# Sliding-window attention with sinks and a top-128 MLP: TensorE's order written by hand, five rotating PSUM banks, early row stores, block-wise ranks, indirect DMA

## The chip, the cores and the metric

The kernel runs on one core of one Trainium2 chip. The metric is the device time of one execution in microseconds (us); lower is better. A core has five engines that run beside each other and wait for each other by semaphores: PE (TensorE, matmuls; its weight loads are shown as PEld), DVE (VectorE), ACT (ScalarE), POOL (GpSimd) and SP (SyncE, which only issues DMAs here). DMAs issued by SP appear in the profile as queue q1 (hardware_dynamic), those issued by POOL as queue q0 (software_dynamic); both run on the same 16 DMA engines.

## What is computed

Four batches (B=4), eight heads, 768 positions, head size 64. First attention, in which each query sees the first 4 keys (sinks) and the last 128 keys; then, per batch, the 128 rows with the highest gate score go through a two-layer MLP and are added back:

```python
keep = is_sink | in_window                       # 4 sinks, window of 128
a = softmax(where(keep, q @ k.T / sqrt(64), -1e9))
x = (a @ v) with the heads side by side          # [4, 768, 512]
scores = x @ w_gate
out = x.copy()
for b in range(4):
    top_idx = the 128 rows with the highest scores[b]
    ye = relu(x[b, top_idx] @ w1) @ w2           # 512 -> 1024 -> 512
    out[b, top_idx] += sigmoid(scores[b, top_idx])[:, None] * ye
```

## The kernel before, in words

The work is cut into 24 units (b, j): batch b, and block j of 128 queries, j = 0 to 5. A block's keys are its own block and the one before it, and the sinks.

- `load_qk` (L68) loads q and k of a batch as bf16 through POOL's DMA queue (qb, kb), `load_v` (L82) loads v (vbuf, six chunks of 256 KB, one per block c) and the sink rows (vsk, eight small pieces). For batch 0, POOL issues q and k in four parts each (L77) and then the six chunks of v (L90); the later v loads are issued by SP.
- `transposes` (L136) turns two heads of kb and qb with 24 matmuls against an identity into PSUM (trp, L145); DVE copies the half with k to KT (L150), ACT the half with q to QT (L152).
- `scores` (L160): eight matmuls per block (L169), for block 0 also mask matmuls (L176); ACT takes the exponential into pt (L179); POOL cuts the window edges by affine selects (L182, L186).
- `pv_sinks` (L198) and `pv` (L207): matmuls with pt as weights and vbuf as the moving operand (L214), with the sinks added by two matmuls (L203); DVE divides (L220, L221) into the tile x, which holds a whole batch.
- `finish_block` (L225): DVE's gate scores (L227) and ACT's bf16 copy xb (L230).
- `moe_gen` (L233), the top-128 part of the batch before, is a Python generator advanced during the units of the next batch: scores are spread over all partitions by a diagonal and a ones matmul (dg L240, bc L241, sbc L243), each block's scores are compared with all 768 (cjunk L250), which gives ranks and a selection matrix E (L253) and its transpose ET (L259, L260); selected rows are gathered by 24 matmuls (xeT L267), the MLP follows (hps L284, hT L286, ye L290, gye L293), six matmuls scatter it back (ops L298), DVE adds x (o_sb L300), and SP stores the whole batch (L303).

Unit u issues the scores of unit u+1, then its own pv, then the transposes for the next batch (units j = 1 to 4). The program text gives these as priorities only: a scheduler sets the order of each engine's instructions and mixes them finely. PSUM has eight banks: two buffers of two banks shared by trp, sc, sk, bc, hps and ops, three buffers for xg, one bank for etp, xeT, se and ye. After the last unit the whole generator of batch 3 runs with nothing beside it.

The order of the work is the loop at the end (L323 to L349), of which these lines matter most:

```python
        if nxt:
...
            for g in range(2):
                scores(states[nxt[0]], nxt[1], g)
        pv_sinks(st, j)
        for g in range(2):
            pv(st, j, g)
            if gen is not None:
                if next(gen, "end") == "end":
...
        finish_block(st, j)
...
        if b + 1 < B and 1 <= j <= HP:
            transposes(states[b + 1], j - 1)
```

## Time and profile before

| | us |
|---|---|
| median of 3 runs | 204.23 (202.47 to 204.92) |
| the profiled execution | 201.09 |
| its span, first to last instruction | 199.4 |
| outside its span | 1.69 |
| PE busy | 157.9 (79%) |
| DVE busy | 121.6 (61%) |
| mean granted clock of TensorE | 0.955 |

The rows below come from that one profiled execution. A row of the timeline gives the start, the time until its last instruction has ended, the engine, the line and the instructions merged into it; the time between the starts of two successive PEld rows is what a group takes of PE's queue.

### The profile page before, as it was taken

The numbers are of one execution on the slowest core, as the hardware profiler recorded it, in microseconds if no ns is written. First come the engines' busy times: TensorE is split into PE (matmuls) and PEld (weight loads), VectorE is DVE, ScalarE is ACT, GpSimd is POOL, SyncE is SP. The second block draws the span as 40 slices with busy tenths as digits, with TensorE's granted clock in tenths as the row PEclk, the third lists the DMA queues.
The fourth block names the chain that finished last, engine by engine and source line by source line (L and its number), as shares of the span: only waits on it lengthen the run. The fifth ranks groups of instructions, "written<-read, shape, count | busy, mean of one in ns | idle before, by whom it ended". The sixth has DMA issues, their size and how long they took to land.

```text
span 199.4 us, 5721 instructions
## 1 busy us (share of the span) xinstructions
PE 157.9 (79%) x2456; PEld 109.7 (55%) x2456; DVE 121.6 (61%) x328; ACT 85.9 (43%) x113; POOL 65.7 (33%) x111
## 2 busy tenths in 40 slices
PE   0023998999997999999979999999799999426640
...
PEclk9999999999999999999999999999978999955995
DMA  5999999999999782480400003500000034000016
GB/s 85 188 230 218 200 191 200 201 197 193 190 191 192 129 182 36 154 271 6 105 5 0 3 0 132 190 0 3 0 3 0 3 140 179 5 0 0 0 64 252
DMA packets 33065, 21.63 MB, mean 108 GB/s; under 512 B 19728, under 2 KB 28944, under 8 KB 33040
## 3 DMA queue, kind: packets, MB, share of 16 engines
...
## 4 chain that ended last, share of the span: by engine, by line
PE 52%; DVE 20%; DMA 9%; POOL 7%; ACT 6%; issue 3%; DVEq 1%; ACTq 0%; POOLq 0%
PE xg L214 18%; DVE cjunk L250 11%; DMA kb<-in_k_dram 9%; PE xg L203 6%; PE ye L290 4%; PE bc L241 4%; PE hps L284 4%; PE trp L145 4%; PE xeT L267 4%; DVE E L253 3%; PE sc L169 3%; PE ops L298 3%; POOL vbuf L90 2%; ACT pt L179 2%; POOL qb L77 2%
## 5 line engine op out<-in xcount | busy, mean ns | idle before, releaser
L214 PE MATMUL xg<-vbuf,pt 128*64 128x65 f32 x1408 | 60.8, 231 | 0.0
L214 PEld LDWEIGHTS xg<-vbuf,pt 128*64 128x64 f32 x1408 | 51.2, 142 | 14.4 <-issue 12.3
L182 POOL TENSOR_SCALAR_AFFINE_SELECT pt<-pt 128x512 f32<-128x512 f32 x40 | 25.6, 641 | 92.9 <-ACT pt L179 92.5
L179 ACT ACTIVATE pt<-sc 128x1024 f32<-128x1024 f32 (+1 forms) x48 | 44.8, 953 | 22.2 <-PE sc L169 15.9
L220 DVE RECIPROCAL rz<-xg 128x4 f32<-128x4 f32 x48 | 8.6, 179 | 35.7 <-PE xg L214 35.5
L230 ACT CAST xb<-x 128x512 bf16<-128x512 f32 x24 | 14.8, 616 | 26.2 <-DVE x L221 26.2
L250 DVE TENSOR_SCALAR_CACHE_REDUCE cjunk<-sbc,scol 128x768 f32<-128x768 f32 x24 | 24.1, 1005 | 2.6 <-ACT sbc L243 2.6
L145 PE MATMUL trp<-ident_b,kb 128*64 128x128 bf16 x192 | 10.2, 244 | 14.7 <-DVE ident_b L104 13.6
L186 POOL TENSOR_SCALAR_AFFINE_SELECT pt<-pt 128x512 f32<-128x512 f32 x32 | 21.0, 656 | 0.0
L221 DVE TENSOR_TENSOR x<-xg,rz 128x256 f32<-128x256 f32 x48 | 20.2, 422 | 1.2
L169 PE MATMUL sc<-QT,KT 64*128 64x256 bf16 (+1 forms) x192 | 19.2, 273 | 0.7 <-ACT pt L179 0.2
L203 PE MATMUL xg<-vsk,psk 32*128 32x260 f32 x64 | 19.6, 429 | 0.0
L300 DVE TENSOR_TENSOR o_sb<-ops,x 128x1024 f32<-128x1024 f32 x12 | 14.5, 1220 | 6.4 <-PE ops L298 6.4
L150 DVE COPY KT<-trp 128x768 bf16<-128x768 bf16 x16 | 15.0, 948 | 4.7 <-PE trp L145 4.7
L227 DVE CUSTOM_DVE_ANT_0 junk<-x,wgb 128x512 f32<-128x512 f32 x24 | 16.8, 700 | 0.3
L145 PEld LDWEIGHTS <-kb 128*64 128x64 bf16 x192 | 8.2, 124 | 15.3 <-DMA kb<-in_k_dram 8.0
L259 PE MATMUL etp<-ident_b,E 128*128 128x128 bf16 x24 | 5.9, 244 | 11.0 <-DVE E L253 10.9
L152 ACT COPY QT<-trp 128x768 bf16<-128x768 bf16 x16 | 12.7, 798 | 3.0 <-PE trp L145 2.5
L145 PE MATMUL trp<-ident_b,qb 128*64 128x128 bf16 x192 | 10.2, 244 | 3.6 <-DVE KT L150 3.5
L145 PEld LDWEIGHTS <-qb 128*64 128x64 bf16 x192 | 8.0, 124 | 7.3 <-issue 7.0
L169 PEld LDWEIGHTS <-KT 64*128 64x128 bf16 x192 | 7.0, 95 | 7.9 <-issue 4.7
L203 PEld LDWEIGHTS xg<-vsk,psk 32*128 32x128 f32 x64 | 8.2, 183 | 5.4 <-issue 3.6
...
## 6 DMA issues: line engine op xcount, KB each, us to landing
...
qb<-in_q_dram POOLq DMA_DIRECT2D x3, 768.0 KB, 18.5
kb<-in_k_dram POOLq DMA_DIRECT2D x3, 768.0 KB, 17.1
...
qb<-in_q_dram POOLq DMA_DIRECT2D x4, 192.0 KB, 5.6
kb<-in_k_dram POOLq DMA_DIRECT2D x4, 192.0 KB, 6.0
```

Source lines behind the costliest of these rows:

```text
L145: nc.tensor.transpose(out=trp[64 * e:64 * e + 64, t, c, :], in_=src[:, 2 * hp + e, c, :], identity=ident_b[:])
L150: nc.vector.tensor_copy(out=o, in_=i)
L169: nc.tensor.matmul(out=sc[:, e, hh, 0:nq], lhsT=st.KT[64 * e:64 * e + 64, hp, kc * 128:(kc + 1) * 128], rhs=st.QT[64 * e:64 * e + 64, hp, ...
L179: nc.scalar.activation(out=po[:, :, :, 0:nq], in_=sc[:, :, :, 0:nq], func=ACT.Exp, scale=0.125)
L182: nc.gpsimd.affine_select(out=pt[:, hs, 0:128], in_=pt[:, hs, 0:128], compare_op=ALU.is_ge, fill=0.0, base=0, pattern=[[0, 4], [1, 128]], ...
L186: nc.gpsimd.affine_select(out=pt[:, hs, 128:256], in_=pt[:, hs, 128:256], compare_op=ALU.is_ge, fill=0.0, base=-1, pattern=[[0, 4], [-1, 1 ...
L203: nc.tensor.matmul(out=st.xg[g][:, :, :], lhsT=st.psk[32 * g:32 * g + 32, (j - 2) * 128:(j - 1) * 128], rhs=st.vsk[32 * g:32 * g + 32, :, ...
L214: nc.tensor.matmul(out=xg[64 * m:64 * m + 64, hh, :], lhsT=st.pt[kc][:, h, off + 64 * m:off + 64 * m + 64], rhs=st.v[:, kc, h, :], start=( ...
L221: nc.vector.tensor_tensor(out=st.x[:, j, 256 * g:256 * g + 256].rearrange("p (h d) -> p h d", h=4), in0=xg[:, :, 0:D], in1=rz[:, :, :].to_ ...
L227: nc.vector.tensor_tensor_reduce(out=junk[:, :], in0=st.x[:, j, :], in1=wgb[:, :], scale=1.0, scalar=0.0, op0=ALU.mult, op1=ALU.add, accum ...
L230: nc.scalar.copy(out=st.xb[:, j, :], in_=st.x[:, j, :])
L250: nc.vector.tensor_scalar(out=cjunk[:, :], in0=sbc[:, :], scalar1=scol[:, c:c + 1], scalar2=0.0, op0=ALU.is_gt, op1=ALU.add, accum_out=ran ...
```

## The change

- TensorE's instructions now stand in the order of the program text (`tc.manual_schedule`); the other engines are still ordered by the scheduler.
- One PSUM pool `ps` of five one-bank buffers serves trp (k and q apart), sc (two per half instead of one of two banks), sk, bc, cs, se, xeT, hps (two) and ye in turn; xg keeps three.
- Start: the identity is made before the loads; k is loaded before q; v of batch 0 is issued by SP instead of POOL, and its chunk c = 0 waits for the fifth load of POOL's queue (k of heads 4 and 5). The transposes and scores of batch 0 alternate.
- x is a tile of one block, four buffers, stored to the output as soon as the unit is done (L253). xb is gone.
- Ranks are built block by block: `compare` of unit u-1 runs in unit u and compares block j with blocks 0 to j only; 15 one-column matmuls (cs) sum the rest once per batch.
- The selected rows are gathered from the output in DRAM by an indirect DMA (L309), and the MLP's result is added to them by a second one (L335). ET, the 24 gather matmuls, the six scatter matmuls and o_sb are gone.

```diff
-    sc_ps = ctx.enter_context(tc.tile_pool(name="sc_ps", bufs=2, space=bass.MemoryType.PSUM))
+    ps = ctx.enter_context(tc.tile_pool(name="ps", bufs=5, space=bass.MemoryType.PSUM))
...
-            for src, dst in ((q, st.qb), (k, st.kb)):
-                nc.gpsimd.dma_start(
+            for src, dst in ((k, st.kb), (q, st.qb)):
+                st.loads.append(nc.gpsimd.dma_start(
...
+            ins = nc.sync.dma_start(out=st.v[:, c, :, 0:D],
+                                    in_=v[b, :, c * 128:(c + 1) * 128, :].rearrange("h p d -> p h d"))
+            if behind_load is not None and c == 0:
+                tc.add_manual_dep(ins.ins, behind_load.ins.name, mybir.DependencyInfo(
+                    mybir.DependencyClass.Sync, mybir.DependencyReason.DATA), reason="order of the first loads")
...
+    ident_f = cp.tile([128, 128], FP32, name="ident_f", tag="ident_f")
+    make_identity(nc, ident_f)
     st0 = load_qk(0, 4)
...
+    load_v(st0, st0.loads[4])
...
+            trp = ps.tile([128, 8, 128], BF16, name="trp", tag="ps")
...
+        sc = [ps.tile([128, 2, 256], FP32, name="sc", tag="ps") for _ in range(2)]
...
-        nc.scalar.activation(out=po[:, :, :, 0:nq], in_=sc[:, :, :, 0:nq], func=ACT.Exp, scale=0.125)
+        for e in range(2):
+            nc.scalar.activation(out=po[:, e, :, 0:nq], in_=sc[e][:, :, 0:nq], func=ACT.Exp, scale=0.125)
...
+            st.x = xp.tile([128, DM], FP32, name="x", tag="x")
...
     def finish_block(st, j):
+        nc.sync.dma_start(out=out[st.b, j * 128:(j + 1) * 128, :], in_=st.x[:, :])
...
-        nc.scalar.copy(out=st.xb[:, j, :], in_=st.x[:, j, :])
-
-
-    def moe_gen(st):
+        st.dg = sp.tile([128, 128], FP32, name="dg", tag="dg")
+        nc.vector.tensor_scalar_mul(out=st.dg[:, :], in0=ident_f[:, :], scalar1=st.scol[:, j:j + 1])
...
+    def compare(st, j):
+        bc = ps.tile([128, 128], FP32, name="bc", tag="ps")
+        nc.tensor.matmul(out=bc[:, :], lhsT=ones_f[:, :], rhs=st.dg[:, :], start=True, stop=True)
+        nc.scalar.copy(out=st.sbc[:, j * 128:(j + 1) * 128], in_=bc[:, :])
+        n = 128 * (j + 1)
+        cm = cmp_p.tile([128, n], BF16, name=f"cm{j}", tag=f"cm{j}")
+        nc.vector.scalar_tensor_tensor(
+            out=cm[:, :], in0=st.sbc[:, 0:n], scalar=st.scol[:, j:j + 1], in1=tie[:, S - n:S],
+            op0=ALU.subtract, op1=ALU.is_gt, accum_out=st.row[:, j:j + 1])
+        st.cm[j] = cm
...
+        cs = ps.tile([128, NB], FP32, name="cs", tag="ps")
+        for c in range(NB - 1):
+            for j in range(c + 1, NB):
+                nc.tensor.matmul(out=cs[:, c:c + 1], lhsT=st.cm[j][:, c * 128:(c + 1) * 128],
+                                 rhs=minus1[:, :], start=(j == c + 1), stop=(j == NB - 1),
+                                 skip_group_check=True)
...
+        nc.vector.tensor_tensor(out=st.row[:, 0:nb1], in0=st.row[:, 0:nb1], in1=behind[:, 0:nb1], op=ALU.add)
+        nc.vector.tensor_tensor(out=st.row[:, 0:nb1], in0=cs[:, 0:nb1], in1=st.row[:, 0:nb1], op=ALU.add)
+        E = mp.tile([128, NB, 128], BF16, name="E", tag="E")
+        nc.vector.tensor_tensor(
+            out=E[:, :, :], in0=iota_f[:, :].unsqueeze(1).to_broadcast((128, NB, 128)),
+            in1=st.row[:, :].unsqueeze(2).to_broadcast((128, NB, 128)), op=ALU.is_equal)
...
+        se = ps.tile([128, 2], FP32, name="se", tag="ps")
         for c in range(NB):
-            nc.vector.tensor_scalar(out=cjunk[:, :], in0=sbc[:, :], scalar1=scol[:, c:c + 1],
-                                    scalar2=0.0, op0=ALU.is_gt, op1=ALU.add,
-                                    accum_out=rank[:, c:c + 1])
-            nc.vector.tensor_scalar(out=E[:, c, :], in0=iota_f[:, :], scalar1=rank[:, c:c + 1],
-                                    scalar2=None, op0=ALU.is_equal)
-            if c == 2:
-                yield
-        etp = mo_ps.tile([128, NB, 128], BF16, name="etp", tag="mo")
-        for c in range(NB):
-            nc.tensor.transpose(out=etp[:, c, :], in_=E[:, c, :], identity=ident_b[:])
-        nc.vector.tensor_copy(out=ET[:, :, :], in_=etp[:, :, :])
-        scol16 = mp.tile([128, NB], BF16, name="scol16", tag="scol16")
-        nc.vector.tensor_copy(out=scol16[:, :], in_=scol[:, :])
+            for t in range(2):
+                nc.tensor.matmul(out=se[:, :], lhsT=E[:, c, :], rhs=rd[:, t, c, :],
+                                 start=(c == 0 and t == 0), stop=(c == NB - 1 and t == 1))
+        idx = sp.tile([128, 1], U32, name="idx", tag="idx")
+        nc.vector.tensor_scalar_add(out=idx[:, :], in0=se[:, 0:1], scalar1=float(b * S))
...
+        rows = out[0:b + 1, :, :].rearrange("b s d -> (b s) d")
+        nc.gpsimd.indirect_dma_start(
+            out=xe[:, :], out_offset=None, in_=rows,
+            in_offset=bass.IndirectOffsetOnAxis(ap=idx[:, 0:1], axis=0))
...
+            nc.tensor.transpose(out=xeT[:, dc, :], in_=xe[:, dc * 128:(dc + 1) * 128], identity=ident_b[:])
...
+        nc.gpsimd.indirect_dma_start(
+            out=rows, out_offset=bass.IndirectOffsetOnAxis(ap=idx[:, 0:1], axis=0),
+            in_=gye[:, :], in_offset=None, compute_op=ALU.add)
...
+    with tc.manual_schedule(engines={mybir.EngineType.PE}):
+        start_state(st0)
+        for g in range(2):
+            transposes(st0, 2 * g)
+            transposes(st0, 2 * g + 1)
+            scores(st0, 0, g)
...
+            pv_sinks(st, j)
             for g in range(2):
-                scores(states[nxt[0]], nxt[1], g)
-        pv_sinks(st, j)
-        for g in range(2):
-            pv(st, j, g)
+                pv(st, j, g)
+            if j == 0:
+                sink_scores(st)
+            if b + 1 < B and 1 <= j <= HP:
+                transposes(states[b + 1], j - 1)
+            if u:
+                pb, pj = units[u - 1]
+                compare(states[pb], pj)
             if gen is not None:
                 if next(gen, "end") == "end":
                     gen = None
-        finish_block(st, j)
-        if j == 0:
-            sink_scores(st)
-        if b + 1 < B and 1 <= j <= HP:
-            transposes(states[b + 1], j - 1)
-        if j == NB - 1:
-            gen = moe_gen(st)
-    for _ in gen:
-        pass
+            finish_block(st, j)
+            if j == 0 and b > 0:
+                gen = moe_steps(states[b - 1])
+        compare(states[B - 1], NB - 1)
+        for _ in moe_steps(states[B - 1]):
+            pass
```

The first place is SP's queue at the start of the program. Before, SP loads the gate weights (wgb), the sink rows of batches 0 and 1 (vsk) and then v of batch 1 (vbuf1); v of batch 0 is in POOL's queue:

```order
L131 DMA wgb_162<-in_moe_w_gate_dram 128x512
L88 DMA vsk0_96<-in_v_dram 4x64 [waits DVE_49]
L88 DMA vsk0_96<-in_v_dram 4x64 x6
L88 DMA vsk0_96<-in_v_dram 4x64 [waits DMAHW0_49]
L88 DMA vsk1_97<-in_v_dram 4x64 [waits DMAHW1_49,DVE_49]
```

Now SP's queue holds v of batch 0 (vbuf0_91), the sink rows (vsk0_93), wgb and v of batch 1 (vbuf1_92); DMASW4 is the semaphore of POOL's fifth load, DMAHW0 to DMAHW7 those of SP's own DMAs, in turn:

```order
L88 DMA vbuf0_91<-in_v_dram 128x8x64
L96 DMA vsk0_93<-in_v_dram 4x64 [waits DVE_49]
L96 DMA vsk0_93<-in_v_dram 4x64 x6
L96 DMA vsk0_93<-in_v_dram 4x64 [waits DMAHW0_49]
L88 DMA vbuf0_91<-in_v_dram 128x8x64 [waits DMAHW1_49]
L88 DMA vbuf0_91<-in_v_dram 128x8x64 [waits DMAHW2_49]
L88 DMA vbuf0_91<-in_v_dram 128x8x64 [waits DMAHW3_49]
L88 DMA vbuf0_91<-in_v_dram 128x8x64 [waits DMAHW4_49]
L155 DMA wgb_177<-in_moe_w_gate_dram 128x512 [waits DMAHW5_49]
L88 DMA vbuf0_91<-in_v_dram 128x8x64 [waits DMAHW6_49,DMASW4_49]
L88 DMA vbuf1_92<-in_v_dram 128x8x64 [waits DMAHW7_49]
```

Only the load with the wait for DMASW4 is chunk c = 0: chunks 1 to 5 and wgb moved ahead of it in the queue, since the other engines' order is still the scheduler's.

The second place is PE in batch 1, in unit (1, 1) of the kernel before. There the transposes of the selection matrix (etp) stand between the pv matmuls of one block (xg):

```order
L214 MATMUL xg<-vbuf_95,pt 64x65 x5
L259 LDWEIGHTS E
L259 MATMUL etp<-ident_b,E 128x128
L214 MATMUL xg<-vbuf_95,pt 64x65 x7
L259 LDWEIGHTS E
L259 MATMUL etp<-ident_b,E 128x128
L214 MATMUL xg<-vbuf_95,pt 64x65 x9
```

Now a block's pv stands in one piece, followed by the 24 transposes for the next batch, the spread of one block's scores (bc) and the step of the top-128 part that is due. These rows are the end of unit (1, 1) with the first of the 15 one-column matmuls cs:

```order
L169 MATMUL trp<-ident_b,qb 64x128
L264 MATMUL bc<-dg,ones_f 128x128
L280 LDWEIGHTS cm_608
L280 MATMUL cs<-minus_168,cm_608 128x1
L280 LDWEIGHTS cm_712
L280 MATMUL cs<-minus_168,cm_712 128x1
```

In every unit of batch 1 and later the order is now: eight scores matmuls of the next unit, two sink matmuls, pv, 24 transposes (units 1 to 4, up to batch 2), bc, one step.

The third place is DVE at the end of the program. Before, the six blocks of batch 3 are compared there one after the other, six pairs like the last two rows here, behind the diagonals of the last blocks (dg):

```order
L240 TENSOR_SCALAR dg_2607<-ident_f_130,scol_2035 128x128 [waits DVE_49,PE_49]
L262 CAST scol16_2635<-scol_2035 128x6
L250 TENSOR_SCALAR cjunk_2612,rank_2611<-sbc_2590,scol_2035 128x768 [waits Activation_49]
L253 TENSOR_SCALAR E_2613<-iota_f_160,rank_2611 128x128 [waits DVE_49]
L250 TENSOR_SCALAR cjunk_2612,rank_2611<-sbc_2590,scol_2035 128x768
```

Now DVE ends with the comparisons of blocks 4 and 5 (cm4, cm5), the gate score of block 5 (L255, two instructions), its diagonal, E in one instruction and the row index:

```order
L248 TENSOR_TENSOR x_2704<-xg_2683,rz_2722 128x256 [waits DVE_49]
L268 SCALAR_TENSOR_TENSOR cm4_2728,row_2152<-sbc_2153,scol_2151,tie_159 128x640 [waits Activation_49]
L255 ISA junk_2743,scol_2151<-x_2704,wgb_177 128x512 [waits DVE_49]
L255 ISA scol_2151 128x1
L284 TENSOR_TENSOR row_2152<-row_2152,behind_164 128x5 [waits DVE_49]
L259 TENSOR_SCALAR dg_2745<-ident_f_97,scol_2151 128x128 [waits DVE_49]
L292 TENSOR_SCALAR rid1_174<-scol_2151 128x6
L293 SCALAR_TENSOR_TENSOR rid1_174<-scol_2151,rid1_174 128x6 [waits DVE_49]
L268 SCALAR_TENSOR_TENSOR cm5_2750,row_2152<-sbc_2153,scol_2151,tie_159 128x768 [waits Activation_49]
L285 TENSOR_TENSOR row_2152<-cs_2752,row_2152 128x5 [waits PE_49]
L287 TENSOR_TENSOR E_2770<-iota_f_157,row_2152 128x768 [waits DVE_49]
L302 TENSOR_SCALAR idx_2787<-se_2774 128x1 [waits DMASW3_49,DMASW2_49,PE_49]
```

Four of the six comparisons moved into the units; cm4 stands ahead of the gate score of the last block.

## Rows read from the trace of the kernel before

**Rows 1.** The page, busy time by engine, then the span in 40 slices.

```profile
PE 157.9 (79%) x2456; PEld 109.7 (55%) x2456; DVE 121.6 (61%) x328; ACT 85.9 (43%) x113; POOL 65.7 (33%) x111
...
PE   0023998999997999999979999999799999426640
...
PEclk9999999999999999999999999999978999955995
DMA  5999999999999782480400003500000034000016
```

**Rows 2.** DMA by queue, 24 to 32 us: packets, MB, share of 16 engines.

```profile
q0 software_dynamic: 1491, 1.14, 90.3%
q1 hardware_dynamic: 1496, 0.38, 36.1%
```

**Rows 3.** DMA by queue, 36 to 44 us.

```profile
q1 hardware_dynamic: 1082, 0.27, 26.5%
```

**Rows 4.** DMA by queue, 70 to 75 us.

```profile
q1 hardware_dynamic: 3695, 0.93, 92.6%
```

**Rows 5.** Timeline 0 to 26 us: start, length, instructions, idle before and its releaser.

```profile
7.17 0.13 PEld L145 LDWEIGHTS <-kb 128*64 128x64 bf16 x1 [7.17 <-DMA kb<-in_k_dram]
...
13.60 1.49 PE L145 MATMUL trp<-ident_b,kb 128*64 128x128 bf16 x24 [13.60 <-DVE ident_b L104]
```

**Rows 6.** Timeline 26 to 64 us.

```profile
27.12 1.00 PE L214 MATMUL xg<-vbuf,pt 128*64 128x65 f32 x14
...
33.72 0.53 PE L145 MATMUL trp<-ident_b,kb 128*64 128x128 bf16 x12 [0.65 <-DMA kb<-in_k_dram]
```

**Rows 7.** Timeline 40 to 44.2 us: what each group takes of the weight-load queue.

```profile
40.80 1.95 PEld L214 LDWEIGHTS xg<-vbuf,pt 128*64 128x64 f32 x64 [0.21 <-issue]
...
42.66 0.40 PEld L145 LDWEIGHTS <-kb 128*64 128x64 bf16 x12
...
43.15 0.11 PEld L169 LDWEIGHTS <-KT 64*128 64x128 bf16 x4
...
43.37 0.30 PEld L203 LDWEIGHTS xg<-vsk,psk 32*128 32x128 f32 x4
...
44.01 0.19 PEld L214 LDWEIGHTS xg<-vbuf,pt 128*64 128x64 f32 x2 [0.34 <-issue]
```

**Rows 8.** Chain that ended last, in order of time: start, length, what.

```profile
47.90 0.54 PE sc L176 x2
...
54.92 0.71 PE bc L241 x4
...
71.33 0.63 PE xg L203 x2
72.19 1.81 PE hps L284 x32
...
95.20 0.71 PE bc L241 x4
```

**Rows 9.** Costliest groups: line, shapes, count, busy us, mean ns, idle before.

```profile
L250 DVE TENSOR_SCALAR_CACHE_REDUCE cjunk<-sbc,scol 128x768 f32<-128x768 f32 x24 | 24.1, 1005 | 2.6 <-ACT sbc L243 2.6
...
L150 DVE COPY KT<-trp 128x768 bf16<-128x768 bf16 x16 | 15.0, 948 | 4.7 <-PE trp L145 4.7
L227 DVE CUSTOM_DVE_ANT_0 junk<-x,wgb 128x512 f32<-128x512 f32 x24 | 16.8, 700 | 0.3
```

**Rows 10.** DMA issues by line: KB each, median us to landing.

```profile
kb<-in_k_dram POOLq DMA_DIRECT2D x3, 768.0 KB, 17.1
...
kb<-in_k_dram POOLq DMA_DIRECT2D x4, 192.0 KB, 6.0
```

**Rows 11.** Timeline 168 to 173 us.

```profile
169.25 0.18 DVE L220 RECIPROCAL rz<-xg 128x4 f32<-128x4 f32 x1 [0.29 <-PE xg L214]
```

**Rows 12.** Timeline 177 us to the end.

```profile
181.51 2.72 PE L267 MATMUL xeT<-E,xb 128*128 128x128 bf16 x24 [0.65 <-DVE ET L260]
...
188.17 1.90 PE L290 MATMUL ye<-w_sb,hT 128*128 128x512 bf16 x8 [1.11 <-ACT hT L286]
```

More of the change, by code (lines that the diff above doesn't have):

```diff
@@ L11 @@
 BF16 = mybir.dt.bfloat16
+U32 = mybir.dt.uint32
 ACT = mybir.ActivationFunctionType
@@ L72, in load_qk @@
         st.kb = qkp.tile([128, H, NB, D], BF16, name="kb", tag="kb")
+        st.loads = []
         n = H // parts
@@ L263, in moe_gen @@
+        nc.gpsimd.indirect_dma_start(
+            out=xe[:, :], out_offset=None, in_=rows,
+            in_offset=bass.IndirectOffsetOnAxis(ap=idx[:, 0:1], axis=0))
         yield
-        xeT = mo_ps.tile([128, 4, 128], FP32, name="xeT", tag="mo")
+        xeT = ps.tile([128, 4, 128], BF16, name="xeT", tag="ps")
         for dc in range(4):
-            for c in range(NB):
-                nc.tensor.matmul(out=xeT[:, dc, :], lhsT=st.xb[:, c, dc * 128:(dc + 1) * 128],
-                                 rhs=E[:, c, :], start=(c == 0), stop=(c == NB - 1))
+            nc.tensor.transpose(out=xeT[:, dc, :], in_=xe[:, dc * 128:(dc + 1) * 128], identity=ident_b[:])
@@ L269, in moe_gen @@
         xeT_sb = mp.tile([128, 4, 128], BF16, name="xeT_sb", tag="xeT_sb")
         nc.scalar.copy(out=xeT_sb[:, :, :], in_=xeT[:, :, :])
-        se = mo_ps.tile([128, 4, 128], FP32, name="se", tag="mo")
-        for c in range(NB):
-            nc.tensor.matmul(out=se[:, 0, 0:1], lhsT=E[:, c, :], rhs=scol16[:, c:c + 1],
-                             start=(c == 0), stop=(c == NB - 1))
-        gt = mp.tile([128, 1], FP32, name="gt", tag="gt")
-        nc.scalar.activation(out=gt[:, :], in_=se[:, 0, 0:1], func=ACT.Exp, scale=-1.0)
@@ L277, in moe_gen @@
-        nc.vector.tensor_scalar_add(out=gt[:, :], in0=gt[:, :], scalar1=1.0)
-        nc.vector.reciprocal(out=gt[:, :], in_=gt[:, :])
         yield
         hT = mp.tile([128, 8, 128], BF16, name="hT", tag="hT")
-        hps = sc_ps.tile([128, 8, 128], FP32, name="hps", tag="sc")
-        for fc in range(8):
-            for dc in range(4):
-                nc.tensor.matmul(out=hps[:, fc, :], lhsT=w1_sb[:, dc, fc * 128:(fc + 1) * 128],
-                                 rhs=xeT_sb[:, dc, :], start=(dc == 0), stop=(dc == 3))
@@ L286, in moe_gen @@
-        nc.scalar.activation(out=hT[:, :, :], in_=hps[:, :, :], func=ACT.Relu)
+        for fq in range(2):
+            hps = ps.tile([128, 4, 128], FP32, name="hps", tag="ps")
+            for f4 in range(4):
+                for dc in range(4):
+                    f0 = (4 * fq + f4) * 128
+                    nc.tensor.matmul(out=hps[:, f4, :], lhsT=w1_sb[:, dc, f0:f0 + 128],
+                                     rhs=xeT_sb[:, dc, :], start=(dc == 0), stop=(dc == 3))
+            nc.scalar.activation(out=hT[:, 4 * fq:4 * fq + 4, :], in_=hps[:, :, :], func=ACT.Relu)
@@ L287, in moe_gen @@
         yield
-        ye = mo_ps.tile([128, DM], FP32, name="ye", tag="mo")
+        ye = ps.tile([128, DM], FP32, name="ye", tag="ps")
         for fc in range(8):
@@ L291, in moe_gen @@
                              start=(fc == 0), stop=(fc == 7))
[L292 removed]
+        gye = mp.tile([128, DM], FP32, name="gye", tag="gye")
         nc.scalar.activation(out=gye[:, :], in_=ye[:, :], func=ACT.Copy, scale=gt[:, 0:1])
[L294 to L305 removed]
+        nc.gpsimd.indirect_dma_start(
+            out=rows, out_offset=bass.IndirectOffsetOnAxis(ap=idx[:, 0:1], axis=0),
+            in_=gye[:, :], in_offset=None, compute_op=ALU.add)
```

137 lines of the change are left out of this document (65 added, 72 removed).

## The prediction

> **What bounds the kernel now.** I read the page first (busy times, then the slices), then the DMA queues by window, the timeline of the start, the chain of waits in the middle and the timeline of the end. The page shows PE busy for 157.9 of 199.4 us, with nines from the sixth slice to the thirty-fourth and low digits on both sides [rows 1]: a start of some 27 us, a middle that PE fills, and an end in which PE mostly waits. The DMA row shows nines from the second to the thirteenth slice, so transfers are short of room for the first 65 us.
>
> *Start.* The first k part lands at 7.17, but PE begins at 13.60, when the identity is there [rows 5]; the first pv starts at 27.12 [rows 6]. *Middle.* The spread of batch 0's scores starts at 54.92 and that of batch 1's at 95.20 [rows 8]: 40.28 us for a batch. *End.* The last pv matmul has ended by 169.25 [rows 11]; from there to 199.4 it is 30.2 us, a chain with nothing beside it.
>
> **The start, changed.** The identity now comes first, so PE can begin at about 7 instead of 13.6, and its transposes and scores of batch 0 follow the loads. Then its fixed order brings pv(0, 0), which needs chunk 0 of v. That chunk is the sixth v load of SP's queue, behind chunks 1 to 5, the sink rows and wgb, as the order shows. So its landing time decides, and PE has nothing else that it may do.
>
> How fast does SP's queue move beside POOL's? From 24 to 32 us both had work: 1,491 packets of q0 and 1,496 of q1, one for one, though q0 moved 1.14 MB (765 bytes each) and q1 0.38 MB (256 bytes each, v's rows of one head) [rows 2]. That is 187 packets/us for q1. Beside the larger packets of the weights and q/k it is 1,082 in 8 us, 135/us [rows 3]. Alone it did 3,695 in 5 us, 739/us [rows 4]. Chunk 1 goes first, nearly alone, and I let it land at about 5 us. Behind it stand four chunks and wgb and chunk 0: 5 x 1,024 + 128 = 5,248 packets, from about 6.5 us. POOL's queue holds q and k of batches 0 and 1 (4,096 packets at the 256 per load that 765-byte packets give, some 650 of them gone by then), then w1 and w2. So 3,450 pairs at 187/us take 18.4 us (to 25); the next 1,500 at 135/us 11 us (to 36); the rest alone 0.4 us; with about 1 to 2 us to land, chunk 0 is there at 39 us. Bounds: 22 us if the queues shared evenly by bytes (below), 43 us if all 5,248 went at 135/us. I take 39, since the one-for-one rows are the same situation.
>
> The Trainium skill (DMA: Bandwidth & Descriptors, "Queues, rings and completion order") says that each DMA engine takes turns between its queues packet by packet. The trace agrees (1,491 to 1,496). By that rule alone, chunk 0 lands at the 39 us above; by an even share of bytes it would be near 20.
>
> So the start goes from 27.12 to 39: +12. k and q of batch 1, which PE waits for at 33.72 before [rows 6], are there by then, at no further cost.
>
> **The middle, counted from PE's groups.** From the starts of successive weight loads [rows 7]: 64 pv records (one block) 1.86 us, 12 transposes 0.49, four scores of 128 columns 0.22, the two sink matmuls side by side 0.64; four scores of 256 columns I take at 0.32. From the chain [rows 8]: two masks 0.54, 32 hps 1.81, four bc records 0.71 (so 0.35 for the two of a block). ye takes 1.90 [rows 12]. The four sink-score matmuls I take at 0.87, cs at 0.5, se and the new xeT at 0.4 each (estimates: one-column matmuls and four transposes are below any group of 12 above). A batch in hand order is then, by units 0 to 5: 2.8, 4.3, 4.8, 4.8, 6.1, 6.4, in sum 29.3 us.
>
> The same from above: 40.28 minus what goes, namely 24 gather matmuls (1.5), six etp (1.4), six ops (1.6) and the second half of four sink pairs that stand apart today, 0.63 each [rows 8] (2.5), plus 1.3 for cs, the longer se and the new transposes: 34.6. The gap between the two is the price of mixing (each of the many short pieces of pv pays a change of operand). I take 32: the hand order removes the mixing, but a fixed order waits where the scheduler would have slipped something in. The waits that I see: KT's copy (948 ns [rows 9]) must be done when the third sc buffer of the next unit is taken, about 1.7 us after pv ends by DVE's queue (0.6 for the division, 0.95 for the copy) against 1.6 us by PE's; and xeT must find the gathered rows, 4 to 5 us after se, where PE arrives after 3.5. DVE itself shrinks: six comparisons of 768 (1,005 ns each [rows 9]) become 2,688 columns in all, about 3.5 us for 6.0, and o_sb goes. The two exponentials of 512 per half cost ACT a little more than one of 1,024, and xb pays for it; ACT and POOL (43% and 33% busy [rows 1]) cover both, with one or two us of slack per unit.
>
> Each indirect DMA sits in POOL's queue between affine selects: the gather waits for idx, and behind it stand the selects of the next block, which pv needs. Bounds for its time: 0 beside PE, and 17.1 us, as the 768 KB k loads took [rows 10]; nearest are the 192 KB parts, 6.0 us in full traffic. With DMA quiet after 65 us [rows 1] I take 4, so a batch loses about 1 us to it.
>
> Batch 0 has no top-128 part: 24.3 by the same sums, plus about 2 for waits and for a slow restart (24 transposes took 1.49 us at the start, 12 took 0.53 later [rows 5, 6]): 26.5 for 26.75 before. Batches 1 and 2: 32 each. Batch 3 up to its last pv: 29.3 less its transposes (3.9), next scores (1.7), ye and the last bc (2.2): 21.5; PE is sparser there, and the granted clock fell in such a stretch before (a 7 and an 8 in the PEclk row near 147 us [rows 1]), so I take 25.
>
> **The end.** From the last pv: division 0.8; cm4, which stands ahead of the gate score, 0.9; gate score 0.7 [rows 9] and accumulator 0.1; dg 0.4; bc and its copy 0.7; cm5 1.1; cs and sum 1.0; E 1.1 (0.95 as KT's copy of the same shape); se and idx 0.8; gather 4.0; xeT and copy 1.1; hps 3.0; second hT 0.6; ye 1.9; gye 0.7; scatter and its landing 5.0; the end of the program 0.5. Sum 24.4, for 30.2. hps is put between 1.81 and twice that: after the wait for the gather the PE is cold, as in the end of today, where the clock row shows fives (the lower level, 1.2 GHz) and 24 xeT matmuls took 2.72 us [rows 1, 12]. With the indirect transfers at 2 and at 8.5 the end is 19 to 32.
>
> **The sum.** 39 + 26.5 + 2 x 32 + 25 + 24.5 = 179 us for a span of 199.4. With the 1.69 outside it 180.7 for 201.09. The median of the runs is 204.23, 1.56% above the profiled execution; at that ratio 183.5.
>
> **Rivals.**
> 1. *Chunk 0 is early.* The Trainium skill (same page, "Issuing engines are not separate DMA queues") says that moving transfers between issuing engines saves only the time to issue them. As a mechanism here: 3.4 MB (q, k, v of batch 0, wgb) at the 0.19 MB/us of 1.52 MB in 8 us [rows 2] are 18 us, chunk 0 is there at about 20, PE then waits some 4 us for k and q of batch 1. Span 179 - 39 + 24 = 164, median 168. Against it: the one-for-one packets.
> 2. *No change.* The mixing was not waste and the ends do not shrink: a batch at 36, batch 3 at 29, the end at 30, the rest as above: 196.5 + 1.7, median 201. For it: PE's slices are full in the middle already [rows 1], and a fixed order can't fill a wait.
> 3. *Slower: the five-bank ring.* Every buffer waits for the release of the fifth before it. If DVE runs late by gate score and comparison, KT's copy comes 0.95 + 0.7 + 1.0 = 2.6 us late in each of the 12 units with transposes [rows 9]: +31, span 210, median 215. It decides from 1.7 us per unit on (20.7 us of gain over 12). Against it: DVE's 121.6 us [rows 1] are 30 a batch, and less the 2.5 of the comparisons at most 28 in a batch of 32.
>
> **How the numbers follow.** The forecast's own range is 172 to 196: chunk 0 from 33 to 42, a batch from 29 to 36, the end from 20 to 30. Chances: forecast 0.68, rival 1 0.12, rival 2 0.12, rival 3 0.08. A measurement of this kernel tells about 2% apart. Faster by over 2% (below 200.1): the forecast, rival 1 and a sixth of rival 2: 0.82; within 2% 0.10; slower 0.08. The range that holds 8 in 10 takes in rival 1's time and the middle of rival 2: 168 to 201.
>
> **What would show it.** Right: PE idle from about 19 to 39 us with a wait on a vbuf load; q0 and q1 one for one in that time; bc of equal blocks about 32 us apart in batches 1 and 2; some 24 us from the last pv to the end. Wrong: pv(0, 0) before 28 us (rival 1); waits of PE on KT's copy of over 1 us in every unit (rival 3); waits of pv on the affine selects behind a gather (then the indirect DMA is dearer than 4 us).

## The result and the profile after

The changed kernel takes 187.3 us (median of 4 runs, 186.81 to 188.99), the kernel before 203.35 (200.2 to 204.92): a ratio of 0.932, 95% interval 0.918 to 0.946. The forecast was 183.5 with 168 to 201. The profiled execution took 188.99 us, its span 187.3, with 1.69 outside. Executions that were over 1.5% longer than the shortest of their kernel, at a lower granted clock, are left out of the ratios but not of the medians; the profiled executions of e1, e2, e4 and e8 are of this kind, 2 to 7% above the shortest, so that lengths read from them are somewhat too long.

The page of the kernel after, in the lines that answer to [rows 1]:

```profile
PE 136.1 (73%) x2412; PEld 102.1 (55%) x2412; DVE 103.9 (55%) x313; ACT 76.5 (41%) x161; POOL 76.2 (41%) x117
...
PE   0377400299999994996999979999989789711930
...
PEclk9999999999999997599999978999996969965585
DMA  5999999969999999596406511410241311142004
```

PE works 21.8 us less than before, DVE 17.7 less. The zeros in PE's sixth and seventh slices are the new wait at the start, and the clock row has new dips in the middle (slices 16, 17, 24, 25, 31 and 33). The stages, from the timeline's start of pv in each block 0 and the end of the last pv:

| stage | before | forecast | after |
|---|---|---|---|
| start, to pv(0, 0) | 27.12 | 39 | 36.38 |
| batch 0 | 26.75 | 26.5 | 27.45 |
| batch 1 | 40.28 | 32 | 36.44 |
| batch 2 | 40.28 | 32 | 32.61 |
| batch 3 to its last pv | 34.8 | 25 | 27.19 |
| end | 30.2 | 24.5 | 27.23 |
| span | 199.4 | 179 | 187.3 |

(Batch 3 of before is what the other stages leave.) The start is 9.3 us longer, batches 1 to 3 are 19 us shorter, the end 3 us. PE's waits in the kernel after, by line, what for, total, times and the longest:

```profile
PE xg L239 <- DMA vbuf<-in_v_dram: 15.4, 1, 15.4
PE xeT L315 <- DMA xe<-out_dram,idx: 8.5, 3, 5.3
PE trp L169 <- DMA kb<-in_k_dram: 7.0, 3, 5.5
PE sc L193 <- DVE KT L174: 4.6, 5, 2.6
PE cs L280 <- DVE cm L268: 2.2, 3, 1.3
```

The first is the wait for chunk 0 of v that the prediction describes. In 24 to 32 us the two queues moved as many packets as each other again, as in [rows 2], though not as many bytes (DMA by queue: packets, MB, share of 16 engines):

```profile
q0 software_dynamic: 1000, 1.28, 90.0%
q1 hardware_dynamic: 1000, 0.41, 28.3%
```

Where batch 1 loses 4.4 us against the forecast is seen on PE's and DVE's timelines (start, length, instructions, idle before and its releaser). PE:

```profile
70.56 0.28 PE L193 MATMUL sc<-QT,KT 64*128 64x256 bf16 x1
73.42 1.01 PE L193 MATMUL sc<-QT,KT 64*128 64x256 bf16 x7 [2.58 <-DVE KT L174]
74.36 1.23 PE L228 MATMUL xg<-vsk,psk 32*128 32x260 f32 x4
75.52 3.73 PE L239 MATMUL xg<-vbuf,pt 128*64 128x65 f32 x64
```

DVE at the same place, and in batch 2 at 102 us:

```profile
67.41 1.38 DVE L268 SCALAR_TENSOR_TENSOR cm<-sbc,scol,tie 128x768 bf16<-128x768 f32 x1
...
71.53 0.42 DVE L248 TENSOR_TENSOR x<-xg,rz 128x256 f32<-128x256 f32 x1 [2.08 <-DMA out_dram<-x]
...
102.23 2.62 DVE L255 CUSTOM_DVE_ANT_0 junk<-x,wgb 128x512 f32<-128x512 f32 x1
...
105.35 1.40 DVE L268 SCALAR_TENSOR_TENSOR cm<-sbc,scol,tie 128x768 bf16<-128x768 f32 x1
```

PE stands 2.58 us for KT: DVE could not write x, since the last store of its buffer had not landed, and KT's copy stands behind that. The 64 pv behind this wait take 3.73 us, where an undisturbed block takes 2.09: the granted clock was 0.66 of full speed from 75.5 to 81.5. In batch 2 the same wait on KT is 1.32 us; there junk took 2.62 us instead of 0.69, beside eight affine selects that POOL ran from 101.89 on, behind the scatter.

Batch 1 loses 1.72 us more at the gather, which no store held back: it started 0.44 us after its index did, as in batches 2 and 3, though the profile names a store. It took 5.7 us to land (81.30 to 87.02; the median of the four is 3.8) while the DMA engines were at 0.8 to 0.9 of their time, and PE stood for its rows:

```profile
80.86 0.16 DVE L302 TENSOR_SCALAR idx<-se 128x1 uint32<-128x1 f32 x1
81.30 1.23 POOL L309 DMA_INDIRECT xe<-out_dram,idx  x1 [3.46 <-DMA out_dram<-x]
87.02 0.40 PE L315 MATMUL xeT<-ident_b,xe 128*128 128x128 bf16 x4 [1.72 <-DMA xe<-out_dram,idx]
88.32 2.09 PE L239 MATMUL xg<-vbuf,pt 128*64 128x65 f32 x64
```

The last row shows that the clock does not fall behind every wait: this block took 2.09 us.

The end, PE's timeline from the spread of the last block's scores, which answers to [rows 12]:

```profile
162.78 0.49 PE L264 MATMUL bc<-dg,ones_f 128*128 128x128 f32 x2 [0.49 <-DVE dg L259]
...
166.38 0.48 PE L299 MATMUL se<-rid,E 128*128 128x2 bf16 x12 [1.25 <-DVE E L287]
172.13 0.61 PE L315 MATMUL xeT<-ident_b,xe 128*128 128x128 bf16 x4 [5.27 <-DMA xe<-out_dram,idx]
173.46 3.57 PE L325 MATMUL hps<-xeT_sb,w_sb 128*128 128x128 bf16 x32 [0.73 <-ACT xeT_sb L317]
176.83 2.74 PE L331 MATMUL ye<-w_sb,hT 128*128 128x512 bf16 x8
```

### The profile page after: what moved, and what is told of

It reads as the page before. It is cut to its first block, busy times and chain, and to the rows that moved or that the text cites. A ratio compares the mean times of both kernels' runs of the same rounds, so it can differ in the third digit from the quotient of the medians.

```text
span 187.3 us, 5738 instructions
## 1 busy us (share of the span) xinstructions
PE 136.1 (73%) x2412; PEld 102.1 (55%) x2412; DVE 103.9 (55%) x313; ACT 76.5 (41%) x161; POOL 76.2 (41%) x117
## 3 DMA queue, kind: packets, MB, share of 16 engines
q0 software_dynamic: 11136, 9.96, 34.8%
## 5 line engine op out<-in xcount | busy, mean ns | idle before, releaser
L239 PE MATMUL xg<-vbuf,pt 128*64 128x65 f32 x1408 | 53.6, 242 | 15.4 <-DMA vbuf<-in_v_dram 15.4
L207 POOL TENSOR_SCALAR_AFFINE_SELECT pt<-pt 128x512 f32<-128x512 f32 x40 | 34.1, 863 | 49.6 <-ACT pt L204 49.5
L204 ACT ACTIVATE pt<-sc 128x512 f32<-128x512 f32 (+1 forms) x96 | 46.3, 572 | 9.6 <-PE sc L193 6.8
L211 POOL TENSOR_SCALAR_AFFINE_SELECT pt<-pt 128x512 f32<-128x512 f32 x32 | 28.2, 889 | 0.0
L335 POOL DMA_INDIRECT out_dram<-gye,idx x4 | 6.4, 1604 | 42.8 <-ACT gye L334 42.8
L255 DVE CUSTOM_DVE_ANT_0 junk<-x,wgb 128x512 f32<-128x512 f32 x24 | 20.2, 842 | 0.1
L268 DVE SCALAR_TENSOR_TENSOR cm<-sbc,scol,tie 128x128 bf16<-128x128 f32 (+5 forms) x24 | 18.6, 776 | 1.4 <-ACT sbc L265 0.6
L265 ACT COPY sbc<-bc 128x128 f32<-128x128 f32 x24 | 6.4, 267 | 16.7 <-PE bc L264 16.7
L228 PE MATMUL xg<-vsk,psk 32*128 32x260 f32 x64 | 12.2, 459 | 0.0
L264 PE MATMUL bc<-dg,ones_f 128*128 128x128 f32 x48 | 11.5, 320 | 0.5 <-DVE dg L259 0.5
L259 DVE TENSOR_SCALAR dg<-ident_f,scol 128x128 f32<-128x128 f32 x24 | 10.3, 430 | 0.2
L325 PE MATMUL hps<-xeT_sb,w_sb 128*128 128x128 bf16 x128 | 9.4, 242 | 0.7 <-ACT xeT_sb L317 0.7
```

Source lines behind the costliest of these rows:

```text
L204: nc.scalar.activation(out=po[:, e, :, 0:nq], in_=sc[e][:, :, 0:nq], func=ACT.Exp, scale=0.125)
L207: nc.gpsimd.affine_select(out=pt[:, hs, 0:128], in_=pt[:, hs, 0:128], compare_op=ALU.is_ge, fill=0.0, base=0, pattern=[[0, 4], [1, 128]], ...
L211: nc.gpsimd.affine_select(out=pt[:, hs, 128:256], in_=pt[:, hs, 128:256], compare_op=ALU.is_ge, fill=0.0, base=-1, pattern=[[0, 4], [-1, 1 ...
L228: nc.tensor.matmul(out=st.xg[g][:, :, :], lhsT=st.psk[32 * g:32 * g + 32, (j - 2) * 128:(j - 1) * 128], rhs=st.vsk[32 * g:32 * g + 32, :, ...
L239: nc.tensor.matmul(out=xg[64 * m:64 * m + 64, hh, :], lhsT=st.pt[kc][:, h, off + 64 * m:off + 64 * m + 64], rhs=st.v[:, kc, h, :], start=( ...
L255: nc.vector.tensor_tensor_reduce(out=junk[:, :], in0=st.x[:, :], in1=wgb[:, :], scale=1.0, scalar=0.0, op0=ALU.mult, op1=ALU.add, accum_ou ...
```

## The experiments

Theory: the late chunk 0 alone sets the start; the order by hand saves the price of mixing; batch 1 is held by late stores, by DVE and POOL, and by the low clock behind waits; the end by the gather. The rivals stand in the expectations. Ratios are to the kernel before, timed on the same chip beside each.

**e1, e2: the start.** e1 lets chunk 0 go first; e2 also puts wgb ahead of it.

```diff
+    wgb = cp.tile([128, DM], FP32, name="wgb", tag="wgb")
+    nc.sync.dma_start(out=wgb[:], in_=moe_w_gate.partition_broadcast(128))
-    load_v(st0, st0.loads[4])
+    load_v(st0)
...
```

> The changed kernel, but chunk 0 of v of batch 0 no longer waits for the fifth load of POOL's queue: it is the first load of SP's queue, and wgb the last of them, behind chunk 5. Theory (the late chunk 0 alone sets the start, 36.38 us, and q0 and q1 share packet by packet): pv(0, 0) starts at about 21.5, since chunk 0 is there at about 8; but wgb now lands where chunk 0 did, at about 36, and bc of unit (0, 0), which stands in PE's fixed order in unit (0, 1) (44.19 in the changed kernel), waits for it until about 37.5. So some 6 to 7 us are gained, about 181 us, with a new wait of some 8 us of PE on dg. Rival A (SP's place in the order doesn't matter, the bytes do): chunk 0 and wgb are both there by 22, gain 15 us, 172. Rival B (the transfers of batch 1 are what the whole first 65 us wait for): gain under 2 us.

> As the run before, with wgb ahead of all loads of v. Theory: pv(0, 0) at about 21.5 and no wait on dg; the chunks of v land every 5.5 us (1,024 packets at 187 per us) from 8 us on, ahead of their units. Batch 0 then ends at about 49 to 52 for 63.8, less what PE waits for k and q of batch 1: gain 9 to 14 us, 174 to 178. Rival (the transfers as a whole are the bound: 200 GB/s until 63 us in the changed kernel): PE starts earlier and waits in batch 1 for its v instead; gain under 4 us.

e1: ratio 0.916 (0.910 to 0.922), under 2% from the changed kernel. pv(0, 0) started at 20.82, and bc of unit (0, 0) waited 13.90 us, until 44.01, behind the gate score, which DVE could start only at 42.84, when wgb had landed: the theory's new wait, longer than forecast.

```profile
42.84 0.69 DVE L255 CUSTOM_DVE_ANT_0 junk<-x,wgb 128x512 f32<-128x512 f32 x1 [20.11 <-DMA wgb<-in_moe_w_gate_dram]
44.01 0.76 PE L264 MATMUL bc<-dg,ones_f 128*128 128x128 f32 x2 [13.90 <-DVE rz L245]
```

e2: 0.934 (0.925 to 0.943), no better than the changed kernel. pv(0, 0) started at 20.09 and batch 0 ran as forecast until 46.7; then PE stood 20.46 us. PE's rows on both sides of that wait:

```profile
46.13 0.60 PE L200 MATMUL sc<-mask,ident_b 128*128 128x512 bf16 x2
67.19 0.61 PE L193 MATMUL sc<-QT,KT 64*128 64x256 bf16 x4 [20.46 <-DVE KT L174]
```

And SP's own timeline, with the stores of x, and DVE's write of x that waits for them:

```profile
47.17 13.92 SPq L88 DMA_DIRECT2D vbuf<-in_v_dram  x5
61.19 1.35 SPq L253 DMA_DIRECT2D out_dram<-x  x2
65.30 0.42 DVE L248 TENSOR_TENSOR x<-xg,rz 128x256 f32<-128x256 f32 x1 [20.99 <-DMA out_dram<-x]
```

SP took 13.92 us to issue five loads of v of batch 1 (each waits for the DMA eight before it, whose semaphore it takes over); the first stores of x stand behind them, at 61.19, and unit (0, 4) needs the buffer of unit (0, 0) at 44. So the start was not the bound by itself: its 16 us moved from a wait on v to a wait on a store. The rivals' sizes were right, but none named the store.

**e3: PE's order back to the scheduler.**

```diff
-    with tc.manual_schedule(engines={mybir.EngineType.PE}):
+    if True:
```

> The changed kernel with PE's order left to the scheduler again; pool, loads, ranks and indirect DMAs as changed. Theory (the fine mixing of the short pieces cost some 2.5 us a batch before): pv in pieces of a few matmuls, 2 to 3 us longer a batch, some 8 us in all: about 195. Rival (a fixed order gains by nothing but waits in places): 187 or below, because the scheduler fills PE's waits on KT, xe and cm (15 us in all in the changed kernel).

Ratio 0.923 (0.916 to 0.930), against 0.918 to 0.946 for the order by hand: the rival's time. Batches 1 and 2 take 33.9 and 33.0 us from sink scores to sink scores, against 36.5 and 32.6 by hand. But the mixing of the kernel before did not come back with the scheduler: only block 0 of batch 0 is cut (pieces of 2, 2, 2, 14 and 12 matmuls), and the pv of the kernel before comes in 84 unbroken pieces, by hand in 24, here in 28 (e10: 29). What the scheduler does do is split pairs of sink matmuls, and then each half takes what the pair takes by hand (0.71):

```profile
109.72 0.70 PE L228 MATMUL xg<-vsk,psk 32*128 32x260 f32 x2
...
111.52 0.70 PE L228 MATMUL xg<-vsk,psk 32*128 32x260 f32 x2
112.15 2.09 PE L239 MATMUL xg<-vbuf,pt 128*64 128x65 f32 x64
```

In batch 2 it pays for this with 31.6 us of PE's work for 30.9, and gets it back with 1.0 us of waits for KT for 4.6. So the order by hand gained nothing measurable over the scheduler's. What mixing costs this run does not show, and what ended it is open: with either order a block's pv no longer has a step of the top-128 part between its halves, and the transposes etp are gone, which no run takes apart.

**e4: stores of x issued by ACT.**

```diff
-        nc.sync.dma_start(out=out[st.b, j * 128:(j + 1) * 128, :], in_=st.x[:, :])
+        nc.scalar.dma_start(out=out[st.b, j * 128:(j + 1) * 128, :], in_=st.x[:, :])
```

> The changed kernel with the stores of x issued by ACT instead of SP, where they stand behind v loads that themselves wait. Theory: the wait of DVE for the store of x (2.08 us at 69.5) and that of the first gather (3.46 us at 77.8) go or shrink to under 1 us, PE's 2.58 us on KT and 1.72 us on xe in batch 1 with them, and the stretch at the lower clock behind them (64 pv in 3.73 us instead of 2.09): batch 1 takes 32 to 33 us instead of 36.4, 184 us. Rival: the stores are late because the DMA engines have no room until 80 us; they land as late from any queue, and issuing them costs ACT time: 187 to 189.

Ratio 0.937 (0.930 to 0.945), no gain. The theory's waits in batch 1, KT of unit (1, 1) and the gathered rows, did go. In their place ACT stood 8.43 us with a store that waited for a vsk load, and PE 7.30 us behind it for pt:

```profile
75.41 0.60 ACT L204 ACTIVATE pt<-sc 128x512 f32<-128x512 f32 x1 [8.43 <-DMA vsk<-in_v_dram]
```

The rival's result, by another way: it was the queue in which ACT's other work stood, not the cost of issuing.

**e5: e2 with 12 buffers of x.**

```diff
-    xp = ctx.enter_context(tc.tile_pool(name="xp", bufs=4))
+    xp = ctx.enter_context(tc.tile_pool(name="xp", bufs=12))
```

> The kernel of e2 (wgb and chunk 0 of v first) with 12 buffers of x instead of 4. In e2 the start moved as forecast (pv(0, 0) at 20.09 instead of 36.38), but at 44.3 DVE waited 20.99 us for a store of x, and PE behind it 20.46 on KT. Theory: that wait is from the ring of four x buffers behind stores that stand in SP's queue behind the v loads of batch 1; with 12 buffers it goes, and what is left is PE's wait for v of batch 1, a few us: 174 to 179. Rival (the transfers themselves are late, 200 GB/s until 63 us): the chunks of v of batch 1, issued from 47 to 61 in e2, hold PE until about 60 whatever DVE does, and the first gather waits for the late stores: 185 to 190, as e2.

184.24 us (181.54 to 185.39), between the theory's range and the rival's. DVE's wait was gone and v of batch 1 cost PE 0.9 us, so that part of the rival falls; but the wait moved on, to the gather of batch 0, which reads those same stores. POOL's timeline:

```profile
75.58 1.03 POOL L309 DMA_INDIRECT xe<-out_dram,idx  x1 [13.73 <-DMA vsk<-in_v_dram]
```

PE's, at the transposes of the gathered rows:

```profile
80.62 0.61 PE L315 MATMUL xeT<-ident_b,xe 128*128 128x128 bf16 x4 [13.16 <-DMA xe<-out_dram,idx]
```

(The releaser named is a load; SP issued the sixth store of batch 0 at 72.57, and the gather started 3.0 us later.)

**e6, e11: the selects left out, and beside.** Neither kernel cuts the window's edges. e6:

```diff
-        if kc > 0:
-            hs = slice(4 * g, 4 * g + 4)
-            nc.gpsimd.affine_select(
...
```

e11 (the second select alike):

```diff
+            cut = cp.tile([128, 4, 256], FP32, name="cut", tag="cut")
             nc.gpsimd.affine_select(
-                out=pt[:, hs, 0:128], in_=pt[:, hs, 0:128], compare_op=ALU.is_ge,
+                out=cut[:, :, 0:128], in_=pt[:, hs, 0:128], compare_op=ALU.is_ge,
```

> The changed kernel without the affine selects of POOL in blocks 1 to 5, so the keys outside the window are not cut there. Theory (DVE's instructions with two SBUF inputs and POOL's selects hold each other up, as when junk took 2.62 us instead of 0.69 beside selects of 1.2 to 1.9 us at 102): junk falls from 842 ns on average to under 720, cm of 768 columns from 1,296 to about 1,020, PE's waits on KT (4.6 us) and on cm (2.2 us) to under 2 us together, and the lower clock behind them goes in batch 2 and 3. Time 182 to 185. Rival (the KT waits come from the store of x and from DVE's order alone): junk and cm as before, waits as before, 187 or what the selects' latency alone gives, about 186.

> The changed kernel with the same affine selects on POOL, reading pt, but writing a tile that nobody reads: POOL is as busy, and pv doesn't wait for it; the keys outside the window are not cut. Theory (DVE and POOL hold each other up): junk about 840 ns, cm of 768 about 1,300, KT waits of PE 2 to 5 us, batches 2 and 3 as in the changed kernel (32.6 and 26 us). Rival (in the run without selects it was pv's wait for the selects that went): batches as in that run, 29.4 and 22 us, though junk is slow.

e6: 181.44 us in one run, though chunk 0 came later (pv(0, 0) at 42.47). Batches 1 and 2 took 30.4 and 29.4 us, batch 3 22.0 from its sink scores to the last pv (26.1 in the changed kernel). Batch 1's gain is not the selects' alone: it began 6.1 us later (sink scores at 71.00 for 64.91), and DVE had no wait for a store of x. DVE's groups by shape (count, then busy us and mean ns of one, then idle before), of the changed kernel:

```profile
L255 DVE CUSTOM_DVE_ANT_0 junk<-x,wgb 128x512 f32<-128x512 f32 x24 | 20.2, 842 | 0.1
L174 DVE COPY KT<-trp 128x768 bf16<-128x768 bf16 x16 | 15.2, 949 | 7.8 <-PE trp L169 7.8
...
L268 DVE SCALAR_TENSOR_TENSOR cm<-sbc,scol,tie 128x768 bf16<-128x768 f32 x4 | 5.2, 1296 | 0.6 <-ACT sbc L265 0.6
```

and without the selects:

```profile
L246 DVE CUSTOM_DVE_ANT_0 junk<-x,wgb 128x512 f32<-128x512 f32 x24 | 16.4, 684 | 0.1
L174 DVE COPY KT<-trp 128x768 bf16<-128x768 bf16 x16 | 15.2, 949 | 8.9 <-PE trp L169 8.9
...
L259 DVE SCALAR_TENSOR_TENSOR cm<-sbc,scol,tie 128x768 bf16<-128x768 f32 x4 | 4.1, 1016 | 0.6 <-ACT sbc L256 0.6
```

junk and cm, which read two tiles of SBUF, are longer by 23% and 28% on average with the selects running; KT's copy, which reads PSUM, is 949 ns in both. The averages hide few long ones: 22 of the 24 junk are at 0.68 to 0.69 us and two at 2.62 and 2.56, each beside a run of eight selects behind a scatter; three cm of 768 beside selects are at 1.38 to 1.40, the fourth, with none beside it, at 1.02. Where a lone select ran beside junk (five times), junk kept its 0.68 to 0.69 and the select took 0.9 to 1.2 us for 0.63.

The Trainium skill (SBUF — State Buffer, "Who interferes with whom") says that a VectorE instruction with two SBUF inputs contends with a GpSimd instruction that reads SBUF, and that one with at most one SBUF input does not, unless it runs in one of VectorE's modes that use two ports. The trace agrees for junk, cm and KT's copy, by these numbers; dg, which reads one tile and a column, is not as clear (430 ns on average for 284).

e11 (188.44 us in one run) was to tell this from pv's wait for the selects and does not: junk came to 734 ns and cm to 1,101, short of the 840 and 1,300 expected, batches 2 and 3 to 30.4 and 24.9 us, between the two kernels, and batch 1 was held by the gather again (3.63 us). How the 3 to 4 us a batch divide stays open.

**e7: batch 3's rows gathered by PE.**

```diff
+        if b == B - 1:
+            xeT = ps.tile([128, 4, 128], FP32, name="xeT", tag="ps")
+            for dc in range(4):
+                for c in range(NB):
+                    nc.tensor.matmul(out=xeT[:, dc, :], lhsT=st.xb[:, c, dc * 128:(dc + 1) * 128],
+                                     rhs=E[:, c, :], start=(c == 0), stop=(c == NB - 1))
...
```

> The changed kernel, but batch 3's rows are gathered by 24 matmuls from bf16 copies of x (as before the change) and only the scatter is an indirect DMA. Theory (at the end the way idx, wait for the scatter of batch 2, gather, landing is on the path: 166.38 for se to 172.12 for xeT, 5.7 us): xeT starts at about 166.4 and takes 1.5 to 2.7 us; the end from the last pv shrinks from 27.2 to 22 to 24 us: 183 to 184. Rival (the end is set by the clock and by POOL: hps and ye run at the lower clock, gye waits for gt, which now comes later): under 2 us, 186.

179.47 us, ratio 0.893 (0.883 to 0.904): twice the gain forecast. The end took 19.8 us instead of 27.2; PE's timeline there:

```profile
163.29 1.51 PE L304 MATMUL xeT<-E,xb 128*128 128x128 bf16 x24 [1.25 <-DVE E L291]
164.64 0.44 PE L311 MATMUL se<-rid,E 128*128 128x2 bf16 x12
165.53 1.95 PE L338 MATMUL hps<-xeT_sb,w_sb 128*128 128x128 bf16 x32 [0.45 <-ACT xeT_sb L307]
167.34 1.90 PE L344 MATMUL ye<-w_sb,hT 128*128 128x512 bf16 x7
```

Not only the 5.27 us of waiting went; hps and ye ran at the higher clock again, 2.5 us less in all.

**e8: PE kept busy at the end.** Matmuls of 512 columns into a tile that is not read:

```diff
+    def keep_busy(n):
+        dum = ps.tile([128, 512], FP32, name="dum", tag="ps")
+        for _ in range(n):
+            nc.tensor.matmul(out=dum[:, :], lhsT=ident_b[:, :], rhs=mask0[:, :, :], start=True, stop=True)
...
```

> The changed kernel with matmuls that nobody reads put into PE's waits at the end: 6 of 512 columns ahead of cs, 5 behind it, 16 behind se. Theory (the granted clock is at its lower level from 164.6 to 178.5 because PE stands): the clock stays up, hps takes 1.9 us instead of 3.57 and ye 1.9 instead of 2.74, so the end is 2 to 3 us shorter: 184.5. Rival (the lower level doesn't follow from PE's idling here): the added matmuls themselves run at the lower clock, 16 of them take 7 us and hold back xeT by 2 us: 189.

At the end the theory held: hps 1.95 and ye 1.90 us, the end 25.5 us instead of 27.2, though the gather still waited for batch 2's scatter. The time does not settle it: 188.95 us (185.79 to 190.39) beside 186.81 to 188.99, with 6.7 us of KT waits in the middle for 4.6, where nothing had been edited.

**e9, e10: the waits taken out together.** e5, with the rows of batches 0 and 3 gathered as in e7; e10 the same in the scheduler's order, by the edit of e3.

```diff
+        if b in (0, B - 1):
+            xeT = ps.tile([128, 4, 128], FP32, name="xeT", tag="ps")
...
```

> The kernel of e5 (wgb and chunk 0 first, 12 buffers of x) with the rows of batches 0 and 3 gathered by 24 matmuls from bf16 copies of x, as in e7 for batch 3; the scatter of batch 0 one unit later. Theory: e5's 13.2 us wait of xeT in batch 1 was for stores of x that are late behind the v loads of SP's queue; without a gather that reads them it goes, and the low clock behind it. From e5's times: pv(1, 0) at 49.9, batch 1 34, batch 2 32.5, batch 3 26, end 20: span 163, median 164 to 168. Rival A: POOL's scatter of batch 0 now waits for the same stores and holds back the selects of batch 2: 172 to 176. Rival B: with the wait gone PE runs into the next late transfer (v or k of batch 2) and nothing is gained on e7: 178 to 181.

> As the run before, with PE's order left to the scheduler. Theory (by e3 the order by hand is worth nothing measurable): within 2% of the run before. Rival: now that PE waits less for transfers, the order by hand shows its worth, 2 us a batch: 6 to 8 us slower than the run before.

e9: 164.7 us (163.8 to 165.57), ratio 0.817 (0.807 to 0.826), as the theory had it. From the starts of the sink scores: batches of 32.0, 31.8 and 34.1 us, the end 19.7. e10: 167.01 us, 0.824 (0.810 to 0.837), the same within the intervals. PE's longest waits in e9:

```profile
PE trp L169 <- DMA kb<-in_k_dram: 7.4, 2, 7.0
PE trp L169 <- DMA qb<-in_q_dram: 3.8, 3, 3.5
PE sc L193 <- DVE KT L174: 2.5, 5, 1.3
```

**e12: e9 with PE kept busy in three waits,** by `keep_busy` of e8.

```diff
+            if st.b == 1 and hp == 0 and t == 1:
+                keep_busy(14)
             trp = ps.tile([128, 8, 128], BF16, name="trp", tag="ps")
...
+        if b in (1, 2):
+            keep_busy(4)
         nb1 = NB - 1
```

> The kernel of e9 (164.7 us) with matmuls that nobody reads put into three waits of PE: 14 of 512 columns ahead of the first qb transposes of batch 1 (a wait of 3.50 us in e9), 4 behind cs in units (2, 1) and (3, 1) (1.32 us on KT and 1.04 on psk). Theory (a stretch at the lower clock follows such a wait: 28 to 34 us and 93 to 99 us in e9, pv of a block 3.14 and 3.73 us instead of 2.09): the clock stays up behind them, 1.5 to 2 us each, two of them: 160.5 to 162.5 us. Rival (the clock falls for another reason, or the added matmuls only shift the wait): no gain, 164 to 166.

162.41 us (159.23 to 166.47), ratio 0.798 (0.787 to 0.810), which just overlaps e9's. The mean granted clock was 0.943 to 0.978 in its six executions, 0.921 to 0.943 in e9's four. The granted clock is 1.00 from 28 to 34 and from 90 to 98 us, where e9's windows from 28 to 32 and from 94 to 98 had 0.50. PE at the first place, in e12:

```profile
24.86 3.20 PE L163 MATMUL dum<-mask,ident_b 128*128 128x512 bf16 x13
28.10 0.53 PE L176 MATMUL trp<-ident_b,qb 128*64 128x128 bf16 x12
...
30.47 2.09 PE L246 MATMUL xg<-vbuf,pt 128*64 128x65 f32 x64
```

In e9 those pv took 3.14 us. At the third place, unit (3, 1), e9 had lost nothing (2.09 us behind a wait of 1.04), so only two places could gain. That matmuls in the wait keep the clock up is shown in these traces; that the time gains by it is likely, not settled.

## Why the prediction was right, and where not

- *Start: right, with errors that offset each other.* 39 was forecast from packets one for one, 36.38 came. The pairs were slower than in the sum from 24 us on (1,000 in 8 us for 1,496), but q1 had a lead by then: it moved 1,485 packets in 8 to 12 us. The sum's own terms (6.5, 18.4, 11.1, 0.4 and 1 to 2) make 37.4 to 38.4 and not 39, and its bound with all 5,248 packets at 135 a us is 45.4 and not 43.
- *Rival 1 was wrong in what it promised.* It took 15 us off for an early chunk 0 (24 for 39). e1 and e2 had pv(0, 0) at 20 and gained under 2%: wgb, then the ring of four x buffers, then the gather were late in turn. "Early row stores" were priced at nothing in the prediction; that was its largest omission (20.46 us of PE in e2), and it hid because chunk 0 was later than all of them.
- *Middle: the step "I take 32" failed for batch 1 (36.44, which rival 2 had at 36) and met batch 2 (32.61) by luck.* The sum from PE's groups, 29.3, was the bare work: e6 shows 30.4 and 29.4, and for batch 3, from its pv(3, 0) at 129.72 to the last pv at 152.83, 23.1 against a bare 21.5. The mixing did go, but "the hand order removes the mixing" named a cause that was not needed: it is as good as gone in the scheduler's order too (e3, e10). The 2.7 us between 29.3 and 32 were left for waits, none of them named with a price. In batch 1 PE stood 4.3 us for KT and the gathered rows, behind a store of x and a gather that was long to land, in batch 2 it stood 1.7 us; the blocks behind KT's wait took 1.6 and 1.4 us longer, at the lower clock. Work of POOL and DVE that hold each other up has a part in it that stays open (e6, e11).
- *KT's copy* was named as the place of a wait, and rival 3 as every unit: it is 4.6 us in five units, two of them behind cm of 768. No pv waited for selects behind a gather.
- *End: 24.5 forecast, 27.23 measured.* Mis-sized were the gather (4.0; idx to xeT 5.2, of which 1.5 is the wait for batch 2's scatter, since the gather reads the tensor that the scatter writes), hps (3.0; 3.57), ye (1.9; 2.7) and scatter with the end (5.5; 6.7).
- *The scale.* 180.7 for the execution was 8.3 short of 188.99; the factor 1.0156 to the median gave 2.8 of it back by chance, and this time the median lay 0.9% below the profiled execution.
